# A new order for all operations of an attention and MLP kernel, and one more batch's Z from f16 parts

## The chip, the cores and the metric

The kernel runs on one core of one Trainium2 chip. The metric is the time of one execution on the device, in microseconds (us); lower is better. The core has five engines that run side by side, each in the order of its own instructions: TensorE (PE in the profile, with its weight loads as PEld), VectorE (DVE), ScalarE (ACT), GpSimd (POOL), and SyncE (SP), which only issues DMA transfers here. An engine waits for another one by semaphores.

## The reference

Two attentions, one after the other, for 8 batches of 8 heads with 576 positions of 64 elements, and then an MLP over the 4608 rows of all batches:

```python
p_packed = sm_attn(p, k, v)                 # 32 packed queries attend to 576 keys
out = sm_attn(q, p_packed, p_packed)        # 576 queries attend to the 32 packed rows
x = out.transpose(0, 2, 1, 3).reshape(B * S, H * D)        # 4608 x 512
h = x @ w_in                                # 512 x 1024
e = np.exp(h - h_max)
solu = h * (e / (e.sum(-1) + 1e-9))
ln = (solu - mu) / np.sqrt(var + 1e-6) * g_ln
result = ln @ w_out                         # 1024 x 512
```

q, k, v, p and g_ln are float32, w_in and w_out float64, the result float32. sm_attn is a softmax of the scaled products, with 1e-9 added to the sum, times the values.

## The kernel before, in words

**Folding.** The second attention's output is never built. Since x @ w_in = (weights of the second attention) @ (p_packed @ w_in), the kernel multiplies the packed rows of a batch by w_in once, which gives Z (256 rows of 8 heads x 32, by 1024), and the first product of the MLP becomes (softmax weights, 576 x 256) @ Z. To keep float32's accuracy at f16 speed on PE, a float32 factor is split into a high and a low f16 part, and a product is the sum of three f16 products (high by high, high by low, low by high).

**A batch.** `attention(b)` (line 396) names its operations, all with /b behind: `lk0`, `lk1` load K with the packed queries in two halves, `lq0`, `lq1` load Q, `lv` loads V. `s10`, `s11` are the scores' two halves on PE, `mx` their row maxima (DVE), `mb` a bias, `ex` the exponentials (ACT), `ri`, `rs` the inverse sums. The exponentials are turned either on PE (`tp0` to `tp2`, copied by `tc0` to `tc2`) for the first three batches or, from `E16` = 3 on, split into f16 parts (`eh`, `el`), turned by a DMA (`et`) and joined (`ea`). `av` is the product with V on PE, `pp` scales it, `pe` and `pk` find its largest value, `pt` turns it on PE and `pc` copies it out; `un` and `uq` set the scales of the batch. `sx0`, `sx1` are the second attention's scores, `sb` a transpose by 32x32 blocks on DVE, and `sm`, `su`, `se`, `ss`, `si`, `sr`, `sn`, `at` the softmax over blocks of 32; `ah`, `al` split the result into f16 parts. Batch 0 does this softmax in two halves (`su0`, `su1` and so on). `z0`, `z1` are the two halves of Z on PE; `zh0`, `zl0`, `zh1`, `zl1` split them into f16 parts on their way out of PSUM.

**Where Z gets its factors.** For b < `Z16` a half of Z is one float32 product of the packed rows with w_in (line 596); from `Z16` on it is three f16 products. That needs w_in in f16 parts, made once (`zw0` to `zw3`, line 258, the high parts; `zy0` to `zy3`, line 261, the low parts, written over the float32 ones), and the batch's packed rows in two parts (`ph`, line 606, and `pl`, line 610). The four `zy` must come after the last float32 Z and before the first f16 Z:

```python
        if b < Z16:
            terms = [(st['ppT'], w_in_sb)]
        else:
            terms = [(st['ph'], w_hi), (st['ph'], w_lo), (st['pl'], w_hi)]
```

**A tile of rows.** `token_tile(i)` (line 693) names the operations of 128 output rows, with -i behind: `m1` is the first product (two PSUM banks; 12 matmuls of 512 columns), `nm` the row maximum (DVE), `nb` a bias, `bd` a bound (two small operations), `ex` the exponential (ACT), `u` the product with h and the sum (DVE), `mu` the mean, `yh` and `yl` the f16 parts of u, `tr` their transpose by DMA, `sq` the sum of squares (ACT), `ca` and `cr` the row's factor (POOL), `m2a` and `m2b` the two halves of the second product (12 matmuls each), `ev` the scaling out of PSUM, `st` the store. Every fifth tile or so lies across two batches and copies their scales first (`uc`).

**The weights.** w_in and w_out arrive as float64 words (`lw0` to `lw3`, `lW0` to `lW3`, 1 MB each), and `wa` (ACT), `wl`, `wm` (DVE) make float32 of them. `wp`, `wb0`, `wb1`, `wb` and `pw0`, `pw1`, `pw` find their scales, `cs` and `cv` the column means of g_ln * w_out, `ct` subtracts them (eight operations on DVE), `ch` and `cl` split the result into f16 parts for the second product. The raw words live in buffers that belong to others later (`W_HOME`, line 28). `hw` are fillers: two matmuls each that nobody reads.

**The order.** `ORDER` (line 29) lists every operation once. `perform` (line 364) issues them in that order, checks that what each needs stands ahead of it and that buffers and PSUM banks are free, and ties the instructions of each engine to one another, so that every engine, SP with its DMAs too, runs its share in exactly this order. A letter behind the colon is the engine of an operation that several could do (v DVE, p POOL, a ACT; without one, the usual engine of that operation), a digit is the first PSUM bank of a matmul group (0 to 5 are three pairs; 6 and 7 single). So `zw3/w:a` is done by ACT and `m1-4:0` writes banks 0 and 1. An operation waits for its inputs, for its engine's operation ahead, and for whoever last held its bank or buffer: a bank pair of `m1-i` is freed by `u-i`, of `sx` by `sb`, of `z` by `zl`, of `s1` by `ex`.

Of the kernel before, what the change touches and what calls it, by code (L numbers as in the profile page):

```python
# [899 lines left out]
```

## Time and profile before

| | |
|---|---|
| median of 3 runs | 377.14 us (377.0 to 378.87) |
| the profiled execution | 375.99 us, its span 374.2 us |
| mean granted clock of PE | 0.986 |
| busy share PE, DVE, ACT, POOL | 95%, 76%, 55%, 58% |
| HBM read, written | 38.80 MB, 9.44 MB |

The span goes from the first to the last instruction; the execution has 1.8 us around it. Times in the views count from the span's start. A busy share is of the time an instruction occupies its engine. Matmuls overlap and their ends are modelled: a row of PE in the chain of waits gives the time by which a group moved its end, and 12 matmuls of 512 f16 columns move it by 2.59 us when they run without a hole. PEclk is the granted clock of PE, 1.00 for 2.4 GHz and 0.50 for 1.2 GHz.

### The profile page before, as it was taken

Reading aid. Unit: us, or ns where it says so; the run is one execution under the profiler, and the core shown is the slowest. Engines: PE = TensorE matmul, PEld = TensorE weight load, DVE = VectorE, ACT = ScalarE, POOL = GpSimd, SP = SyncE. Lnnn points to the kernel's source line nnn. Section 1 sums busy time; section 2 is a strip of 40 time slices with the busy share of each in tenths; the row PEclk is TensorE's granted clock in tenths of the full one; section 3 lists DMA queues with packets and bytes.
Section 4 is the critical chain, followed back from the end, with each engine's and each line's share of the span. In section 5 each row is a group of like instructions: output and inputs, shape, how many; then the busy total and the mean of one; then the engine's idle time right before and its main releaser. Section 6 shows DMA issues by size and latency. Waiting matters only on the chain.

```text
span 374.2 us, 7628 instructions
## 1 busy us (share of the span) xinstructions
PE 356.7 (95%) x3013; PEld 168.1 (45%) x3013; DVE 283.5 (76%) x419; ACT 206.9 (55%) x346; POOL 218.1 (58%) x315
## 2 busy tenths in 40 slices
...
GB/s 288 420 424 428 310 261 194 276 284 208 347 184 238 254 141 197 265 234 191 91 145 152 196 80 107 122 163 70 170 56 0 134 93 87 168 52 145 114 197 57
DMA packets 99349, 70.56 MB, mean 189 GB/s; under 512 B 88049, under 2 KB 88049, under 8 KB 97777
## 3 DMA queue, kind: packets, MB, share of 16 engines
...
q8 instruction: 23, 0.38, 0.4%
...
HBM read 38.80 MB, written 9.44 MB: 129 GB/s over the span
## 4 chain that ended last, share of the span: by engine, by line
PE 69%; DVE 13%; DMA 7%; POOL 4%; ACT 3%; issue 3%; SPq 1%; ACTq 0%; DVEq 0%; POOLq 0%
PE pa L789 32%; PE ps L723 20%; PE ps L789 8%; DMA yT<-yhl 4%; DMA v<-in_v_dram 3%; PE ps L604 2%; PE pa L504 2%; POOL yhl L763 2%; PE ps L436 2%; PE ps L538 1%; DVE w_in_sb L199 1%; DVE yhl L323 1%; DVE u L752 1%; DVE nm L729 1%; DVE zl L622 1%
## 5 line engine op out<-in xcount | busy, mean ns | idle before, releaser
L789 PE MATMUL pa<-wch,yT 128*128 128x512 f16 x416 | 129.2, 379 | 1.6 <-DMA yT<-yhl 1.6
L789 PEld LDWEIGHTS <-yT 128*128 128x128 f16 x864 | 83.6, 98 | 104.0 <-DMA yT<-yhl 3.4
L789 PE MATMUL pa<-wcl,yT 128*128 128x512 f16 x208 | 78.8, 379 | 0.0
L763 POOL TENSOR_TENSOR yhl<-u,yhl 128x1024 f16<-128x1024 f32 x22 | 48.6, 2207 | 20.1 <-ACT yhl L148 11.1
L729 DVE TENSOR_REDUCE nm<-ps 128x1 f32<-128x1024 f32 x36 | 43.8, 1218 | 19.1 <-PE ps L723 17.3
L752 DVE SCALAR_TENSOR_TENSOR u<-e,s_row,ps 128x1024 f32<-128x1024 f32 x36 | 45.4, 1270 | 16.4 <-ACT e L747 10.5
L747 ACT ACTIVATE e<-ps,bias,unit 128x1024 f32<-128x1024 f32 x36 | 43.3, 1202 | 23.1 <-DVE bias L144 21.3
L723 PE MATMUL ps<-zh,a2h 128*128 128x512 f16 (+1 forms) x160 | 54.8, 381 | 0.5 <-DVE rs L465 0.5
L723 PE MATMUL ps<-zl,a2h 128*128 128x512 f16 (+1 forms) x160 | 54.6, 379 | 0.0
L723 PE MATMUL ps<-zh,a2l 128*128 128x512 f16 (+1 forms) x160 | 54.6, 379 | 0.0
L789 PE MATMUL ps<-wch,yT 128*128 128x512 f16 x160 | 49.6, 379 | 0.0
L723 PEld LDWEIGHTS <-a2h 128*128 128x128 f16 (+1 forms) x320 | 27.7, 100 | 35.7 <-issue 4.7
L771 ACT ACTIVATE e<-u,negmu 128x1024 f32<-128x1024 f32 x36 | 41.1, 1141 | 3.4 <-POOL negmu L144 2.6
L148 ACT CAST yhl<-u 128x1024 f16<-128x1024 f32 x22 | 22.9, 1041 | 19.5 <-DMA yT<-yhl 13.0
L740 POOL TENSOR_SCALAR bound<-nm,unit 128x1 f32<-128x1 f32 x25 | 13.4, 536 | 33.5 <-DVE nm L729 33.4
L781 POOL TENSOR_SCALAR c_row<-sq,k_out,s_eps 128x1 f32<-128x1 f32 x36 | 19.6, 544 | 19.6 <-ACT e L771 19.2
L789 PE MATMUL ps<-wcl,yT 128*128 128x512 f16 x80 | 30.3, 379 | 0.0
L142 ACT ACTIVATE o_sb<-pa,c_row 128x512 f32<-128x512 f32 x17 | 11.6, 683 | 32.3 <-PE pa L789 24.1
L782 POOL TENSOR_TENSOR c_row<-c_row,neg_half 128x1 f32<-128x1 f32 x36 | 21.3, 590 | 3.0
L775 POOL TENSOR_SCALAR s_eps<-se,s_row 128x1 f32<-128x1 f32 x36 | 13.3, 369 | 16.2 <-DVE s_row L742 8.7
L723 PEld LDWEIGHTS <-a2l 128*128 128x128 f16 (+1 forms) x160 | 14.3, 100 | 16.8
L763 DVE TENSOR_TENSOR yhl<-u,yhl 128x1024 f16<-128x1024 f32 x14 | 19.9, 1424 | 0.1
...
## 6 DMA issues: line engine op xcount, KB each, us to landing
...
```

The costliest lines, as they stand in the source:

```text
L148: nc.scalar.copy(out, in_)
L723: nc.tensor.matmul(h[rows, 512 * n:512 * n + 512], lhsT=lhsT, rhs=z[:, r, 512 * n:512 * n + 512], start=t == 0, stop=t == end)
L729: nc.vector.tensor_reduce(out=nm, in_=st['h'], axis=AX.X, op=ALU.max, negate=True)
L740: eng.tensor_scalar(out=bound, in0=st['nm'], scalar1=st['nm'], scalar2=st['unit'][:, 2:3], op0=ALU.mult, op1=ALU.max)
L747: nc.scalar.activation(st['e'], st['h'], AF.Exp, bias=st['bias'], scale=st['unit'][:, 1:2], accum_out=st['se'])
L752: nc.vector.scalar_tensor_tensor(out=st['u'], in0=st['e'], scalar=st['s_row'], in1=st['h'], op0=ALU.mult, op1=ALU.mult, accum_out=st['su'])
L763: engines[on(f'yl-{i}', 'v')].tensor_tensor(out=st['y'][:, 1], in0=st['u'], in1=st['y'][:, 0], op=ALU.subtract)
L771: nc.scalar.activation(st['e'], st['u'], AF.Square, bias=st['negmu'], accum_out=st['sq'])
L775: nc.gpsimd.tensor_scalar(out=s_eps, in0=st['se'], scalar1=1e-09, scalar2=st['s_row'], op0=ALU.add, op1=ALU.mult)
L781: nc.gpsimd.tensor_scalar(out=c_row, in0=st['sq'], scalar1=k_out[:, 0:1], scalar2=s_eps, op0=ALU.mult, op1=ALU.add)
L782: nc.gpsimd.tensor_tensor(out=c_row, in0=c_row, in1=neg_half, op=ALU.pow)
L789: nc.tensor.matmul(st['po'], lhsT=st['yT'][:, a, c], rhs=w[:, c], start=c == 0 and t == 0, stop=c == NFC - 1 and t == 2)
```

## The change

All 1119 words of ORDER change their places, many their engine or bank, and two words come in (`ph/2`, `pl/2`); there are nine fillers instead of ten. `Z16` goes from 3 to 2, so that batch 2's Z is made of three f16 products too, which needs the four `zw` and `zy` ahead of `z0/2`. The loads stand in another order: the second part of w_in ahead of the first K, V ahead of K's second half for batch 1, the rest of w_in ahead of w_out, Q of batch 1 ahead of batch 3's K. The functions stay as they are. The diff, cut to the start, the stretch with the four `zy`, and the end:

```diff
-Z16 = 3
+Z16 = 2
...
 ORDER = '''
-hw28/w:6 lg/w lw0/w lk0/0 s10/0:0 mx0/0 lk1/0 s11/0:2 lk0/1 hw42/w:7 lk1/1 mb0/0:p wa0/w lv/0 hw23/w:6 hw18/w:7 mx1/0
-mb1/0:v wl0/w:v wm0/w lq0/0 lq1/0 lW0/w ex0/0 ex1/0 lw2/w lw1/w tp0/0:6 tp1/0:7 tp2/0:0 tc0/0:v s10/1:4 ri/0:a tc1/0:a
-tc2/0:v av/0:6 mx0/1 mb0/1:p ex0/1 s11/1:2 rs/0 pp/0:v pt/0:7 pe/0 pc/0:a sx0/0:0 mx1/1 sx1/0:4 mb1/1:a sb0/0 sb1/0
-sm0/0 ex1/1 ri/1:p tp0/1:6 tp1/1:0 sm1/0 su1/0:v wl4/w:v tp2/1:1 hw40/w:2 wa4/w tc0/1:a su0/0:p se0/0 ss0/0 si0/0:v gx/w
-se1/0 wa2/w wl2/w:a sr0/0 sn0/0:p wm4/w cs0/w:6 wp4/w:3 wl1/w:a wp0/w:2 wm2/w lw3/w wa1/w at0/0 ss1/0 lW2/w wm1/w pk/0
-wa3/w tc1/1:a wl3/w:v lW1/w wm3/w tc2/1:v wl6/w:v cs1/w si1/0:p wp1/w wa6/w wp2/w wp3/w hw37/w:0 wb0/w wb1/w wl5/w:a
-rs/1 wm6/w lW3/w sr1/0 wa5/w z0/0:4 wa7/w z1/0:0 wb/w un/0 zh1/0:a cs4/w sn1/0:p cs5/w wm5/w wp5/w wp6/w wl7/w:v at1/0
-cs2/w cs3/w zh0/0:a wm7/w zl1/0 wp7/w pw0/w zl0/0 cs6/w pw1/w pw/w cs7/w ah1/0:a ah0/0:a lv/1 al0/0:p al1/0:p ko/w lk0/2
-s10/2:0 mx0/2 lk1/2 cv/w:a av/1:7 s11/2:4 m1-2:2 mb0/2:a pp/1:a ex0/2 ct0/w lk0/3 ct1/w ch0/w:a lk1/3 mx1/2 m1-1:0
-mb1/2:a uq/0 gd/w ct4/w ct5/w ct2/w ex1/2 tp0/2:6 ct3/w nm-2 ch2/w:a cl0/w:p ch1/w:a m1-0:4 nb-2:a ex-2 ri/2:a pe/1
-bd-2:p nm-1 nb-1:v lk0/4 cl1/w:p pt/1:7 bd-1:v ex-1 ca-1 u-2 pk/1 tc0/2:a u-1 mu-1:p pc/1:a ct6/w yh-1:a rs/2 tp1/2:6
-lq0/1 sx0/1:2 tc1/2:a lq1/1 m1-3:0 yl-1:p sq-1 ct7/w nm-0 nb-0:a tp2/2:6 tc2/2:a bd-0:p sb0/1 ex-0 sx1/1:2 nm-3 bd-3:p
-lv/2 sb1/1 u-0 un/1 av/2:6 nb-3:a ex-3 lk1/4 z0/1:2 ch3/w:a s10/3:4 zh0/1:a pp/2:a u-3 tr-1 m2a-1:7 cl2/w:p cl3/w:p
-lq0/2 yh-3:a yl-3:p sm/1 su/1:v se/1 mx0/3 mb0/3:a lv/3 ex0/3 pe/2 s11/3:0 mx1/3 mb1/3:a ex1/3 ss/1 mu-0:p cr-1 zl0/1
-pt/2:6 pc/2:a si/1:p m2b-1 sr/1 sn/1:v at/1 ev-1:a eh/3:a z1/1:4 zh1/1:a uq/1 uc-4 tr-3 yh-2:a ah/1:a yh-0:a el/3:p
...
-el/4:p m2b-0 ev-2:a u-5 ca-5 ex-7 u-7 rs/3 s10/5:2 z0/2:4 mx0/5 av/3:7 tr-4 z1/2:0 tr-6 ev-0:v mb0/5:a si/2:p sr/2 ex0/5
-zh1/2:a zw1/w:p pp/3:v zl1/2 sn/2:p at/2 yh-8:a yl-8:v st-0 s11/5:2 mx1/5 mu-7:a yh-7:a yl-7:p m2a-4:6 zh0/2:a zl0/2
-pt/3:7 pc/3:v pe/3 cr-6 m2a-6:0 m2b-4 zw0/w:a zy0/w et/4 m2b-6 ca-8 lq0/4 ea/4:p st-2 pk/3 mb1/5:a un/3 mu-8:a sq-8
-sx0/3:4 ah/2:a lq1/4 al/2:p sb0/3 ex1/5 tr-7 eh/5:a ev-6:a el/5:p sx1/3:2 s10/6:0 uq/3 sb1/3 ri/4:a ev-4:a mx0/6 rs/4
-mb0/6:a ex0/6 s11/6:4 mx1/6 sm/3 av/4:7 su/3:v pp/4:a mb1/6:v ex1/6 m1-9:2 nm-9 bd-9:v ca-7 sq-7 cr-7 lk0/7 yh-5:v
-yl-5:p m1-11:0 lv/5 nb-9:a ph/3:a tr-8 cr-8 se/3 st-4 nm-11 nb-11:a ex-11 ss/3 bd-11:p m2a-7:6 si/3:p ca-11 zy3/w u-11
-zw2/w:p ex-9 u-9 zy1/w m1-10:4 nm-10 mu-5:v pt/4:7 et/5 m2b-7 yh-9:a yl-9:p m2a-8:0 bd-10:p tr-5 m1-12:2 eh/6:v el/6:v
-m2b-8 nb-10:a mu-9:p m2a-5:1 lq0/5 ev-7:v nm-12 ri/5:a pc/4:a mu-11:v pe/4 bd-12:p sr/3 sn/3:p zy2/w nb-12:v pk/4 tr-9
...
-tr-33 st-27 ca-34 cr-34 tr-31 ca-35 m2a-33:6 m2b-33 ev-28:a st-28 m2a-31:7 u-35 yh-35:v yl-35:v st-25 tr-35 ev-34:v
-m2b-31 ev-33:a st-33 mu-31:p mu-35:v yh-32:v yl-32:p tr-32 m2a-35:6 m2b-35 m2a-32:0 ca-32 m2b-32 sq-35 ca-31 mu-32:v
-sq-31 cr-31 st-34 ev-31:v st-31 cr-35 ev-35:a st-35 hw32/w:7 hw36/w:6 hw8/w:7 hw13/w:6 sq-32 cr-32 ev-32:a st-32 zz/7
+lg/w hw1/w:6 lw0/w hw25/w:7 gx/w wa0/w wl0/w:v wm0/w lw2/w wa2/w wl2/w:a lk0/0 hw9/w:6 s10/0:0 mx0/0 lk1/0 s11/0:2
+mb0/0:v ex0/0 mx1/0 mb1/0:a ex1/0 lk0/1 lv/0 hw10/w:7 lk1/1 tp0/0:6 tp1/0:7 tp2/0:0 lq0/0 lq1/0 s10/1:4 lw1/w lw3/w
+lW0/w lW2/w tc0/0:a wm2/w ri/0:a rs/0 lW1/w tc1/0:a tc2/0:a av/0:6 pp/0:v pe/0 s11/1:2 pt/0:7 mx1/1 pc/0:a mx0/1 sx0/0:0
+sb0/0 sm0/0 mb0/1:p ex0/1 lW3/w hw29/w:6 su0/0:p sx1/0:0 sb1/0 sm1/0 su1/0:p wl1/w:v mb1/1:a ex1/1 tp0/1:6 tp1/1:0 pk/0
+se0/0 wa1/w tc0/1:a ss0/0 si0/0:a wa3/w wm1/w hw2/w:1 tc1/1:a wp0/w:6 wp1/w wp2/w tp2/1:2 wl3/w:v sr0/0 sn0/0:p se1/0
+wm3/w wp3/w at0/0 wb0/w wb1/w tc2/1:a ss1/0 wb/w z0/0:4 z1/0:0 si1/0:p sr1/0 sn1/0:p wl4/w:a wa4/w wm4/w wa6/w wl6/w:a
+ri/1:p un/0 wm6/w ah0/0:a uq/0 wa5/w wl5/w:v wm5/w cs0/w:6 cs1/w wp4/w:7 lk0/2 cs4/w cs5/w cs2/w zh0/0:a zw3/w:p at1/0
+cs3/w lk1/2 wp5/w s10/2:2 zl0/0 wl7/w:a wp6/w wa7/w rs/1 zh1/0:a wm7/w mx0/2 ah1/0:a lv/1 wp7/w pw0/w al0/0:p al1/0:p
+s11/2:4 pw1/w zl1/0 lq0/1 lq1/1 pw/w mx1/2 cs6/w cs7/w cv/w:a mb0/2:a ko/w gd/w ct0/w ct1/w ct4/w mb1/2:a m1-1:0 ct5/w
+nm-1 ex0/2 av/1:7 m1-2:2 lk0/3 bd-1:p ct2/w ex1/2 ri/2:p ch0/w:a pp/1:a ct3/w ct6/w ch2/w:a nb-1:a ch1/w:a cl1/w:p ex-1
+ct7/w tp0/2:6 lv/2 nm-2 tc0/2:a bd-2:p u-1 m1-3:4 nm-3 nb-2:a ex-2 u-2 tp1/2:7 cl2/w:p pt/1:6 tc1/2:a pc/1:a yh-1:a
+tp2/2:7 bd-3:p yl-1:p pe/1 s10/3:0 mu-1:a tc2/2:a mx0/3 sq-1 mb0/3:a sx0/1:2 sb0/1 ex0/3 rs/2 ch3/w:a pk/1 un/1 lk1/3
+lk0/4 av/2:7 pp/2:v cl0/w:p sx1/1:2 sb1/1 ca-1 nb-3:a s11/3:0 mx1/3 ex-3 mb1/3:a pt/2:6 sm/1 m1-0:2 lq0/2 u-3 nm-0
+su/1:p lk1/4 bd-0:p ex1/3 eh/3:a tr-1 lq1/2 yh-3:a yl-3:p nb-0:v z0/1:0 z1/1:4 cl3/w:v cr-1 se/1 tr-3 ss/1 m2a-1:7
+zh0/1:a zl0/1 zh1/1:a lk0/5 el/3:p et/3 ex-0 pc/2:a zl1/1 si/1:a sr/1 m2b-1 ev-1:a s10/4:0 s11/4:4 u-0 yh-0:a mx0/4 ca-3
+m2a-3:7 sn/1:v pe/2 yl-0:p pk/2 m2b-3 ca-2 mu-3:a mb0/4:a ex0/4 mu-2:a at/1 ah/1:a mx1/4 mb1/4:a al/1:v sx0/2:2 sb0/2
+uq/1 sx1/2:0 ex1/4 un/2 sb1/2 ea/3:p ri/4:v m1-4:4 uc-4 nm-4 ri/3:a sm/2 eh/4:a zz/0 el/4:p bd-4:v zw1/w:a sq-3 cr-3
+nb-4:v ex-4 yh-2:v yl-2:p mu-0:p sq-2 tr-0 m1-7:2 nm-7 ev-3:a u-4 st-1 ca-0 nb-7:a rs/3 lv/3 ex-7 bd-7:v lk1/5 lq0/3
+zy1/w u-7 su/2:p yh-4:a m2a-0:6 mu-7:p m1-8:0 sq-0 cr-0 ca-7 s10/5:4 mx0/5 tr-2 av/3:7 zw2/w:a se/2 nm-8 mb0/5:a bd-8:p
+lq1/3 yl-4:p m2b-0 ev-0:a st-3 zy3/w yh-7:a ex0/5 lv/4 m1-6:2 pp/3:v pt/3:7 uq/2 ss/2 si/2:p nm-6 nb-8:a m2a-2:6 ex-8
+ca-8 s11/5:4 yl-7:v u-8 mu-8:v cr-2 sq-7 mu-4:a tr-7 sq-4 mx1/5 m2b-2 pe/3 ph/2:a nb-6:a ex-6 pk/3 zy2/w zw0/w:v ev-2:a
+pl/2 zy0/w tr-4 bd-6:p m1-5:0 nm-5 et/4 pc/3:v mb1/5:a ex1/5 u-6 lk0/6 m2a-7:6 lk1/6 yh-8:a st-0 z0/2:4 z1/2:2 zh0/2:a
+yl-8:p un/3 ph/3:a sq-8 sr/2 sn/2:v at/2 m2a-4:7 m2b-7 nb-5:a ea/4:v bd-5:p cr-7 m2b-4 uq/3 lk0/7 yh-6:v zh1/2:a zl1/2
+sx0/3:2 st-2 mu-6:v ah/2:a al/2:p eh/5:a ex-5 u-5 zz/1 ev-7:a lq0/4 yl-6:p av/4:6 rs/4 zl0/2 sb0/3 sx1/3:0 el/5:p
+s10/6:4 pp/4:a sb1/3 sm/3 tr-6 ca-4 mx0/6 mu-5:a s11/6:2 ca-5 mx1/6 lv/5 m1-9:0 cr-4 pl/3 ev-4:a st-4 m2a-6:6 nm-9
...
+yh-32:v m1-35:2 ca-28 m2a-30:7 tr-33 nb-34:a ex-34 mu-28:a sq-28 cr-28 m2a-33:0 bd-34:v u-34 ca-34 ev-28:a st-28 cr-30
+m2b-30 m1-31:4 zz/7 yh-34:v yl-34:p m2b-33 yl-32:v tr-34 uc-31 nm-31 tr-32 m2a-34:6 ev-30:v ca-32 nm-35 nb-35:v sq-32
+nb-31:v ev-33:v m2b-34 cr-32 m2a-32:7 ex-35 mu-34:p sq-34 zz/6 st-33 bd-35:p u-35 bd-31:p mu-35:p st-30 yh-35:v cr-34
+ca-35 yl-35:v m2b-32 ex-31 tr-35 m2a-35:0 m2b-35 u-31 yh-31:a ev-34:a st-34 yl-31:v tr-31 m2a-31:6 mu-31:v sq-31 m2b-31
+sq-35 cr-35 ev-35:a ev-32:v st-32 hw33/w:7 hw27/w:7 st-35 hw31/w:7 ca-31 cr-31 ev-31:a st-31
 '''
```

## Rows read from the trace of the kernel before

**Rows 1.** The page: busy us, share and instructions of each engine.
```profile
PE 356.7 (95%) x3013; PEld 168.1 (45%) x3013; DVE 283.5 (76%) x419; ACT 206.9 (55%) x346; POOL 218.1 (58%) x315
```

**Rows 2.** Windows by stage: from:to, length, busy us of each engine, clock, DMA.
```profile
0.00:46.43 46.43, 35.81 (x438) 21.48 (x442) 31.99 (x66) 24.61 (x34) 10.09 (x23) 0.89 0.92 377
46.43:67.28 20.85, 17.36 (x245) 8.17 (x235) 20.59 (x34) 17.46 (x34) 15.15 (x17) 1.00 0.75 224
67.28:82.04 14.76, 14.76 (x149) 6.21 (x151) 13.80 (x15) 12.55 (x22) 12.28 (x16) 1.00 0.84 288
82.04:109.45 27.41, 27.41 (x266) 12.67 (x264) 23.42 (x36) 19.66 (x36) 22.96 (x36) 1.00 0.89 246
109.45:124.24 14.79, 14.65 (x212) 7.08 (x197) 13.54 (x17) 11.35 (x18) 13.65 (x10) 1.00 0.95 258
124.24:370.46 246.22, 244.95 (x1737) 111.89 (x1734) 180.10 (x256) 120.59 (x202) 143.93 (x218) 1.00 0.57 135
370.46:374.20 3.74, 1.73 (x9) 0.59 (x6) 0.00 (x0) 0.69 (x1) 0.00 (x0) 1.00 0.18 70
```

**Rows 3.** Waits of PE: line, waited for, us in total, times, longest.
```profile
PE ps L604 <- DVE u L752: 0.7, 1, 0.7
```

**Rows 4.** Chain of waits, in order of time: start, us, what.
```profile
3.92 11.45 DMA v<-in_v_dram
...
62.00 5.21 DMA yT<-yhl
...
82.06 5.41 PE ps L723 x36
...
106.24 0.86 PE ps L604 x16
...
108.35 1.10 PE ps L604 x16
...
124.28 5.29 PE ps L723 x24
...
153.12 1.44 PE ps L604 x46
```

**Rows 5.** Timeline of the start: start, us, engine, line, operation, tiles, shapes, idle before.
```profile
7.86 0.72 PE L436 MATMUL ps<-kT 64*32 64x288 f32 x16 [1.27 <-DMA kT<-in_k_dram]
...
12.93 0.68 DVE L150 COPY e1T<-pa 128x512 f32<-128x512 f32 x1
...
17.59 1.21 PE L436 MATMUL ps<-kT 64*32 64x288 f32 x16
17.71 0.61 DVE L144 TENSOR_SCALAR pp<-pa,rs 128x128 f32<-128x128 f32 x2 [3.16 <-PE pa L504]
...
23.44 1.16 DVE L566 TENSOR_TENSOR s<-s,mx 128x576 f32<-128x576 f32 x1
...
24.52 0.68 DVE L188 TENSOR_SCALAR u<-kT 128x1024 int32<-128x1024 int32 x1
...
46.43 1.41 DVE L323 SCALAR_TENSOR_TENSOR yT<-yT,gs,o_sb 128x512 f32<-128x512 f32 x2
```

**Rows 6.** Groups by line: tiles, shapes, count, busy us, mean ns, idle before.
```profile
L763 DVE TENSOR_TENSOR yhl<-u,yhl 128x1024 f16<-128x1024 f32 x14 | 19.9, 1424 | 0.1
...
L262 DVE SCALAR_TENSOR_TENSOR w_in_sb<-w_in_sb,w_pow,w_hi 128x1024 f16<-128x1024 f32 x4 | 7.1, 1779 | 0.0
...
L144 DVE TENSOR_SCALAR zh<-ps 128x1024 f16<-128x1024 f32 x5 | 6.1, 1220 | 7.5 <-PE ps L604 7.5
...
L144 POOL TENSOR_SCALAR w_hi<-w_in_sb,w_pow 128x1024 f16<-128x1024 f32 x2 | 5.7, 2871 | 0.1
...
L612 DVE SCALAR_TENSOR_TENSOR pl<-ppT,unit,ph 128x256 f16<-128x256 f32 x5 | 2.6, 513 | 0.0
```

**Rows 7.** Windows of the start in which PE's clock was granted at half.
```profile
15.77:19.19 3.42, 3.42 (x94) 2.17 (x82) 1.17 (x4) 0.00 (x0) 0.00 (x0) 0.50 1.02 419
...
26.00:32.84 6.84, 5.21 (x21) 3.06 (x22) 6.74 (x12) 5.95 (x7) 3.07 (x2) 0.50 1.01 413
```

70 lines of the change are left out of this document (33 added, 37 removed).

## The prediction, made before the change was run

> **What bounds the kernel now.** I read the page's busy line first, then the windows by stage, then the waits of TensorE (PE), then the timeline and the chain of waits where those pointed. The busy line puts PE at 95% and VectorE (DVE) at 76% of the span [rows 1], an average that hides three stages [rows 2]. Up to 67.28 us PE has holes (35.81 of 46.43 us and 17.36 of 20.85 us busy, and some of that is slow or overlapping matmuls) while DVE is nearly full in the second piece (20.59 of 20.85). From 67.28 to 124.24 PE has 0.14 us of idle time and DVE is 89% busy: 13.80 + 23.42 + 13.54 = 50.76 of 56.96 us. From 124.24 to 370.46 PE is idle for 246.22 - 244.95 = 1.27 us, over half of it in the one wait of [rows 3], and DVE has a quarter of its time free. The last 3.74 us are one scaling and one store. So the time is: where the dense stretch begins, plus a fixed amount of matmuls, plus small stalls, plus a tail. Nothing that moves work off ScalarE (ACT) or GpSimd (POOL) late in the kernel can be worth more than 1.27 us; the startup and the DVE load up to 124 us decide.
>
> **Two checkpoints.** I counted each engine's operations in both orders. When m1-4 begins (82.06 us before [rows 4]) PE has run exactly the same matmuls in both, fillers aside. When m1-9 begins (124.28 us) it has run one second product, m2-7, in place of another, m2-6: the same amount. At m1-9 the durations of the operations listed ahead sum to 107.7 us on DVE before and 107.8 after, 99.2 and 99.2 on ACT, 68.1 and 70.1 on POOL (164, 143 and 98 instructions in the trace up to there; the sums overcount by up to 4%, DVE's busy time up to there being 31.99 + 20.59 + 13.80 + 23.42 + 13.54 = 103.3 us [rows 2]). So the change is judged by when PE reaches these two points.
>
> **Part A: DVE's load before m1-4 falls by 2.5 us.** Leaving DVE for ACT or POOL, or moved behind: one of batch 0's subtractions su1/0 (1.16), three weight shifts wl4, wl6, wl7 (0.68 each), the copies tc0/0 (0.68) and tc2/0, tc2/1 (0.28 each), four operations of 0.15 to 0.42 us (0.96), and su/1 (1.36): 6.8 us. Arriving: wl1, wl5 (0.68 each), pp/2 (0.61), four small ones (0.98) and cl3: 2.95 + cl3 [rows 5]. A subtraction of cl3's shape has no row on DVE; yl on DVE has the same shape and type (1.42), and a PSUM read of that size is 1.22 [rows 6]; I take 1.3 of 1.2 to 1.5. Sum: 4.25 - 6.8 = -2.5 us. The work goes to ACT, which has 46.43 - 24.61 us free in the first stretch, and to POOL, with 36 us free [rows 2]. Both run in order: zw3, now on POOL at 2.87 [rows 6], stands ahead of al0/0 and al1/0; I get al1/0 done at 42.7 us against m1-1's turn at 45.1, so it is hidden by 2.4 us; gone that cover, m1-1 is late by what is over.
>
> **Part B: batch 0 starts later, +1.0 us.** The second 1 MB of w_in (lw2) now goes ahead of the first K. At 419 GB/s [rows 7] it takes 2.5 us, so K's wait, which ended at 7.86 [rows 5], ends at about 10.3. V, landed at 3.92 + 11.45 = 15.37 [rows 4], gets 2.45 us of lw2 ahead and loses K1's second half (0.59 MB, 1.4 us): 16.4. The first pp/0 on DVE moves from 17.71 [rows 5] to about 18.7. In exchange wm2 is done before it, and lw1, lw3 land ahead of the four pieces of w_out. Bounds: 0 if DVE uses the early weights fully, +2.5 if K's delay goes all the way through; 1.0 is the V path, which ends last.
>
> **Walking the chain with these numbers.** From pp/0 at 18.7 DVE has 26 us of listed work up to the scale pw, and waits about 1.5 us (for wa3, sn0/0, wb1): the first ct at 46.2, before 46.43 [rows 5]. m1-1 starts at 45.1, m1-2 at 48.9, m1-3 at 52.2. nm-1 now stands ahead of the last four ct, so u-1 ends at 56.0, yh-1 at 58.5, yl-1 at 60.7 and its transpose, 5.21 as at 62.00 [rows 4], at 66.0. PE meanwhile does s11/3, pt/2 and z1/1 too (2 us that came after m2a-1 before), the last waiting for u-3's bank until 66.1, and begins m2a-1 at 67.4 (before 67.25). m2a-3 must wait for its transpose (yl-3 behind bd-0 on POOL, landing about 74.6), which gives back 0.5 to 0.7 us of the lead. On SP the Q loads of batch 1 pass ahead of K3; Q, K and V all land before their turn in this walk. m1-4 then starts at 81.0: A, B and this wait are -2.5 + 1.0 + 0.5 = **-1.0 us**.
>
> **Part C: batch 2's Z in f16, -0.5 us on PE.** A half of Z in float32 takes 0.86 to 1.10 (x16), two f16 halves 1.44 together [rows 4]: 2 x 0.97 - 1.44 = -0.5. It adds ph/2 on ACT (0.5) and pl/2 on DVE (0.51), and z0/2 now waits for both and for the four zy, 1.78 us each [rows 6], on DVE, which stand after z1/2 in the order now and ahead of it then. zw0 goes to DVE, for which there is no row: between 0.68 (tc0, half its columns [rows 5]) and 1.22 (zh, as many from PSUM [rows 6]); I take 0.9. Queued behind a late z0/2 on PE are z1/2, m2a-4, m2b-7 and all that follows. Between m1-4 and m1-9 DVE thus has 40.9 us of listed work instead of 38.7, in 41.7 us instead of 42.2; its idle time there, 42.20 - 23.42 - 13.54 = 5.2 us now, falls to about 2.5. By the walk zy0 ends at 108.3 and PE arrives at z0/2 at 109.8: hidden, by 1.5 us. At m1-9 the last bank is freed at 122.4 and PE comes at 122.7.
>
> **The rest: 0.** From m1-9 on PE has the same work. The shortest stretch of PE work between a first product and its second product late in the kernel is 17 us (m1-29; 18 for m1-31), against 13 before (m1-35); the latency of that path is nm 1.2, exp 1.3, u 1.3, two halves 2.3 and the transpose 3.7 to 5.2, 10 to 12 us. Bounds: -1.0 (all stalls gone) to +3 (two of them each as long as a half transpose). The last tile changes from 32 to 31, but what follows the last matmul is still one scaling and one store: 3.74 us [rows 2]. Three fillers in place of four lie beside that store.
>
> **Sum.** -1.0 - 0.5 = -1.5 us on the profiled execution: span 374.2 to 372.7, 375.99 to 374.5 with the 1.8 us around the span. The median of the runs, 377.14, is 1.15 above that execution: **375.6 us**.
>
> **The clock.** PE was granted half of its clock, 1.2 GHz, from 15.77 to 19.19 and from 26.00 to 32.84 [rows 7], the first time right after it had waited for V until 15.37; s1 took 1.21 us in it instead of 0.72 [rows 5]. I kept half the clock for batch 0's product with V, so the sum holds what a drop there costs. The Trainium skill's page "TensorE: Matmul & The Clock Gate", section "HAM oscillation — how this bites in real kernels", describes short bursts of matmuls between waits for DMAs that start at the lower clock each time. The drop at 15.77 agrees with it, and it speaks against this change, whose wait for the first K grows: that is rival 2.
>
> **Rivals.**
> 1. *Only Z counts.* DVE works off its list as late as before; A and B cancel: 377.14 - 0.5 = 376.6. For it: both orders carry 107.8 us of DVE work up to m1-9. Against: the lighter list before m1-4. 0.12.
> 2. *The lower clock comes earlier.* With an idle stretch of 3 us in place of 1.27 ahead of the first K, PE falls to 1.2 GHz before s1: the first s1 (+0.5), the turns (+0.3, in the same ratio) and some of the weights' products come later on DVE's path, about +1.1: 376.7. 0.04.
> 3. *DVE can't take the four zy so early* (the other side). Place: z0/2. If no zy finds a hole in DVE's list, 7.1 - 1.5 = 5.6 us of stall, 381.2; if DVE only keeps the idle time it has now in this stage, zy0 ends 2.7 us later, 1.2 over the margin, 376.8. I take 379.8. It decides from a PE wait at z0/2 to m1-9 of over 3.4 us in all. For it: DVE is 94% full there in the walk. Against: four of DVE's large operations of this stage go to POOL and two to ACT. 0.22.
> 4. *K's delay goes through.* B is +2.5, and A is lost in ACT's queue: 377.14 + 2.5 - 0.5 = 379.1. For it: ACT's list up to the first ct grows by 1.5 us. Against: DVE has the second weight to work on while it waits. 0.07.
> 5. *More gain.* The listed DVE durations overcount by 4%, 4 us by m1-9, so the walk is late by up to 2 us wherever DVE leads: 375.6 - 2.0 = 373.6. Against: the transposes and PE's own work then hold m1-4. 0.25.
>
> **How the numbers follow.** The forecast has 0.30, with its own range of 374 to 377. About 0.5% (1.9 us) is what a measurement of this kernel can tell from no change: under 375.25 is faster, over 379.03 slower. Faster: rival 5 and two fifths of the forecast, 0.25 + 0.12 = 0.37. Slower: rival 4, two thirds of rival 3 and a tenth of the forecast (late stalls), 0.07 + 0.15 + 0.03 = 0.25. Same: 0.38. The range goes from rival 5 with 1.6 us beyond it to most of rival 3's upper end: 372.0 to 380.3.
>
> **What would show it.** In the profile after: K's first wait ending near 10.3; the first ct near 46; m2a-1 near 67.4; m1-4 near 81.0 and m1-9 near 122.7; no PE wait over 1 us at z0/2. Wrong if m1-4 starts after 82, if DVE work holds PE between z0/2 and m1-9, or if PE's idle time after m1-9 is over 3 us.

## The result, and the profile after the change

The changed kernel takes 372.78 us (median of 4 runs, 372.56 to 374.12) beside 377.07 us for the kernel before (376.07 to 378.87): 0.9888 of its time, 95% interval [0.9844, 0.9933]. That is faster than the 375.6 us that were forecast: a gain of 4.3 us beside a forecast one of 1.5. It lies inside the range, 0.8 us above its lower end of 372.0. Its profiled execution took 372.9 us, span 371.1.

The page's busy line, the windows by stage, PE's longest wait and pieces of the chain, all of the changed kernel; columns as in [rows 1 to 4].

```profile
PE 354.9 (96%) x3027; PEld 165.9 (45%) x3027; DVE 278.9 (75%) x421; ACT 209.1 (56%) x357; POOL 214.7 (58%) x304
```

```profile
0.00:47.32 47.32, 35.41 (x388) 19.31 (x389) 30.38 (x61) 26.72 (x41) 17.40 (x26) 0.93 0.97 396
47.32:66.95 19.63, 18.61 (x316) 9.38 (x315) 19.44 (x34) 18.63 (x38) 15.98 (x16) 1.00 0.61 217
66.95:80.67 13.72, 12.94 (x121) 5.54 (x117) 11.93 (x14) 11.14 (x21) 13.14 (x15) 1.00 0.73 172
80.67:122.66 41.99, 41.99 (x481) 19.59 (x477) 37.25 (x59) 30.08 (x52) 37.08 (x43) 1.00 0.85 255
122.66:367.38 244.72, 244.70 (x1733) 111.69 (x1734) 179.93 (x258) 121.85 (x207) 131.11 (x207) 1.00 0.56 140
367.38:371.07 3.69, 1.29 (x6) 0.39 (x4) 0.00 (x0) 0.69 (x1) 0.00 (x0) 1.00 0.18 71
```

```profile
PE ps L436 <- DMA kT<-in_k_dram: 4.0, 2, 3.4
```

```profile
74.19 2.76 PE pa L789 x12
...
80.70 5.41 PE ps L723 x36
...
109.83 1.44 PE ps L604 x48
...
122.66 2.72 PE ps L723 x12
```

What to see: m1-4 begins 1.36 us earlier (80.70 for 82.06 [rows 4]); m1-9 at 122.66 for 124.28; the stretch behind it is 244.72 us for 246.22 [rows 2], with 0.02 us of idle time on PE where there were 1.27; the wait of [rows 3] is gone, and after 75 us PE has no wait worth a row. The tail is the same. 1.36 + 0.26 + 1.5 = 3.1 us is the difference of the spans.

The changed kernel ran again in two later sets of runs (e4, e12 below). These are its checkpoints beside those of the experiments, from the starts of the first matmuls of m1-4 and m1-9 and the end of the last second product in each trace (us):

| | m1-4 | m1-4 to m1-9 | m1-9 to the last product | median of runs | ratio to before |
|---|---|---|---|---|---|
| before | 81.98 | 42.23 | 246.25 | 377.07 | 1 |
| after | 80.63 | 42.00 | 244.75 | 372.78 | 0.9888 |
| e4 (after) | 79.68 | 42.01 | 244.90 | 372.05 | 0.9870 |
| e12 (after) | 80.53 | 42.01 | 244.64 | 372.22 | 0.9882 |
| e1 new head, old tail | 81.80 | 43.86 | 246.50 | 377.99 | 1.0026 |
| e2 old head, new tail | 87.24 | 42.01 | 245.24 | 379.19 | 1.0053 |
| e3 old, two waits removed | 82.53 | 42.22 | 245.68 | 376.23 | 0.9977 |
| e5 old engines in the start | 94.05 | 42.01 | 245.43 | 386.73 | 1.0230 |
| e6 first K ahead | 81.22 | 42.00 | 244.69 | 372.38 | 0.9860 |
| e7 float32 Z | 79.63 | 44.67 | 247.47 | 379.35 | 1.0052 |
| e8 fillers | 79.57 | 42.01 | 245.02 | 372.52 | 0.9856 |
| e9 float32 Z, zy in the holes | 80.42 | 44.00 | 246.71 | 376.52 | 0.9993 |
| e10 wb0 ahead | 80.02 | 42.01 | 244.55 | 372.48 | 0.9886 |
| e11 wb0 ahead, fillers | 80.92 | 42.00 | 245.04 | 373.43 | 0.9910 |

A ratio has an interval of some 0.25 to 0.45% to either side, so the small steps are read from the traces. The first three columns are of the one execution that was profiled, the last two of all runs.

### The profile page after: what moved, and what is told of

Its sections match the earlier page's. It is cut to its first block, busy times and chain, and to the rows that moved or that the text cites. A ratio compares the mean times of both kernels' runs of the same rounds, so it can differ in the third digit from the quotient of the medians.

```text
span 371.1 us, 7650 instructions
## 1 busy us (share of the span) xinstructions
PE 354.9 (96%) x3027; PEld 165.9 (45%) x3027; DVE 278.9 (75%) x421; ACT 209.1 (56%) x357; POOL 214.7 (58%) x304
## 4 chain that ended last, share of the span: by engine, by line
PE 83%; DVE 7%; DMA 6%; POOL 3%; issue 1%; ACT 0%; SPq 0%; POOLq 0%
PE pa L789 41%; PE ps L723 23%; PE ps L789 8%; DMA qT<-in_q_dram 4%; PE ps L604 3%; PE ps L538 2%; PE pa L316 1%; PE pa L504 1%; DMA zh<-in_moe_w_in_dram 1%; POOL wcl L329 1%; PE ps L436 1%; DVE u L752 1%; DVE zl L622 1%; DVE nm L729 1%; DVE yT L323 1%; POOL s L586 1%
## 5 line engine op out<-in xcount | busy, mean ns | idle before, releaser
L789 PE MATMUL pa<-wch,yT 128*128 128x512 f16 x480 | 149.5, 379 | 0.8 <-ACT yhl L148 0.8
L789 PE MATMUL pa<-wcl,yT 128*128 128x512 f16 x240 | 91.0, 379 | 0.0
L763 POOL TENSOR_TENSOR yhl<-u,yhl 128x1024 f16<-128x1024 f32 x23 | 51.2, 2227 | 21.2 <-ACT yhl L148 9.8
L740 POOL TENSOR_SCALAR bound<-nm,unit 128x1 f32<-128x1 f32 x22 | 18.9, 859 | 27.1 <-DVE nm L729 27.0
L789 PE MATMUL ps<-wch,yT 128*128 128x512 f16 x96 | 30.2, 379 | 0.0
L142 ACT ACTIVATE o_sb<-pa,c_row 128x512 f32<-128x512 f32 x22 | 14.9, 684 | 25.9 <-POOL c_row L782 9.2
L148 ACT CAST yhl<-u 128x1024 f16<-128x1024 f32 x20 | 20.7, 1041 | 15.3 <-DVE u L752 13.0
L781 POOL TENSOR_SCALAR c_row<-sq,k_out,s_eps 128x1 f32<-128x1 f32 x36 | 14.8, 411 | 20.1 <-ACT e L771 19.4
L775 POOL TENSOR_SCALAR s_eps<-se,s_row 128x1 f32<-128x1 f32 x36 | 14.5, 402 | 15.3 <-ACT e L747 12.2
L763 DVE TENSOR_TENSOR yhl<-u,yhl 128x1024 f16<-128x1024 f32 x13 | 17.6, 1354 | 2.3 <-ACT yhl L148 2.2
L789 PE MATMUL ps<-wcl,yT 128*128 128x512 f16 x48 | 18.2, 379 | 0.0
## 6 DMA issues: line engine op xcount, KB each, us to landing
kT<-in_k_dram SPq DMA_DIRECT2D x8, 576.0 KB, 10.3
```

The costliest lines, as they stand in the source:

```text
L142: nc.scalar.activation(out, in_, AF.Copy, scale=scale)
L148: nc.scalar.copy(out, in_)
L740: eng.tensor_scalar(out=bound, in0=st['nm'], scalar1=st['nm'], scalar2=st['unit'][:, 2:3], op0=ALU.mult, op1=ALU.max)
L763: engines[on(f'yl-{i}', 'v')].tensor_tensor(out=st['y'][:, 1], in0=st['u'], in1=st['y'][:, 0], op=ALU.subtract)
L781: nc.gpsimd.tensor_scalar(out=c_row, in0=st['sq'], scalar1=k_out[:, 0:1], scalar2=s_eps, op0=ALU.mult, op1=ALU.add)
L789: nc.tensor.matmul(st['po'], lhsT=st['yT'][:, a, c], rhs=w[:, c], start=c == 0 and t == 0, stop=c == NFC - 1 and t == 2)
```

## The experiments

### Halves of the two orders: e1, e2, and the whole again, e4

e1 takes the words ahead of m1-4 from the new order and the others, with their engines and banks, from the old one; e2 the other way round.

```diff
 e1: new order up to m1-4 | then lv/3 mu-0:p uc-4 yh-2:a yl-2:p ... m1-4:0 tr-2 nm-4 ... (old), Z16 = 3
 e2: old order up to m1-4 | then et/3 un/2 ea/3:p ri/4:v m1-4:4 nm-4 ... (new), Z16 = 2
```

> The words ahead of m1-4 in the new order, with the new engines; from m1-4 on the old order and engines, and batch 2's Z in float32. Theory (three parts that add: the start 1.4 us, Z 0.2, late stalls 1.5): m1-4 begins at 80.6 us as in the changed kernel, the tail keeps the waits of 0.5 us ahead of m1-18 and 0.7 us ahead of z1/7, span 372.8, ratio to before 0.996. Rival (one cause: the early start puts VectorE's list ahead, and the late waits go with it): m1-4 at 80.6, no late wait, span 371.5 or less, ratio 0.992. Second rival (all of it is in the tail): m1-4 at 82, span 374.2.

> The words ahead of m1-4 in the old order; from m1-4 on the new order and engines, and batch 2's Z of f16 parts. Theory: m1-4 at 82.0 us, no PE wait after it, 290.5 us from there to the end, span 372.5, ratio to before 0.9955; with the run above the two reductions add up to that of the whole change. Rival (one cause, the early start): with the old start VectorE is 1.4 us later against the same list, so waits come back in the tail, above all at z0/2 (the four zy) and span is 374 or more. Second rival (all of it is in the tail): 371.1.

> The changed kernel itself, again, as the yardstick for the two halves. Theory (the spans tell the gain, and the profiled execution of the kernel before was a lucky one by some 1.1 us): ratio 0.9917, that is -3.1 us. Rival (the runs gain more than the profiled executions): ratio 0.9888, -4.2 us.

None of the theories on the halves came true as a whole: e2 is slower than either whole kernel, and e1 can't be told from the kernel before (1.0026, interval 0.9999 to 1.0054). Waits of PE after 70 us in e1 (the first fence) and in e2, and last the wait that is left in e2 after 124.3 us:

```profile
PE ps L723 <- DVE s L560: 1.8, 1, 1.8
PE pa L789 <- DMA yT<-yhl: 1.5, 1, 1.5
...
PE ps L723 <- DVE rs L465: 0.8, 1, 0.8
PE ps L604 <- DVE u L752: 0.7, 1, 0.7
```

```profile
PE pa L789 <- DMA yT<-yhl: 3.1, 2, 2.5
PE ps L723 <- DVE unit L252: 1.1, 1, 1.1
...
PE pa L789 <- DMA yT<-yhl: 0.6, 1, 0.6
```

In e1 the new head reaches m1-4 at 79.98, and then m1-4 waits 1.8 us: the old order gives it banks 0 and 1, which the new head has just used for sx1/2, and sb1/2 must read them first. Then m2a-2, which the old order has early, waits 1.5 us for a transpose that the new head has not begun. In e2 un/2 stands between VectorE's old list and m1-4 (1.1 us), after a wait of 2.5 us for a transpose. Its m1-4 is 5.3 us later than that of the kernel before, and these waits are not all of it: PE's granted clock was 0.50 from 58.25 to 61.66 and from 78.73 to 82.14 in this execution, where the kernel before has 1.00, and two products there took 4.12 and 4.45 us (m1-3 at 58.82, m2a-3 at 77.92) instead of 2.6 to 2.7. Four other runs of e2, at a mean clock of 0.991, have a median of 378.3 us, beside 376.0 of the kernel before at the same clock, so a loss of some 2.3 us is left. The seam thus costs more than either half brings, and the two runs can't show whether the halves add up. The stretch behind m1-9 does follow its own order, wherever it begins: the old tail takes 246.50 us in e1 with its two waits, now 0.8 and 0.7 us, and the new one 245.24 in e2 with one of 0.6. That part of the first theory stands: the tail's 1.5 us go with the tail's order, and not with the start.

e4, at 0.9870 [0.9825, 0.9915], lies beyond both theory (0.9917) and rival (0.9888), and only the rival's value is inside the interval: against the 376.5 us of before's runs beside it, 4.5 us are gained, while its own span is 3.9 us shorter than the one of [rows 2]. The runs gain more than the two profiled executions show, as the rival said; two reasons, an offset and the clock, are told in the section on the prediction.

### The late waits: e3

```diff
-... sx0/5:0 cr-14 ev-14:v ri/6:p sb0/5 av/6:7 ...
+... sx0/5:0 sb0/5 cr-14 ev-14:v ri/6:p av/6:7 ...
-... ex-27 bd-27:v u-27 ca-27 m2a-25:5 ev-22:a pl/7 nm-28 ah/7:a ... ca-30 nb-28:v ex-28 ...
+... ex-27 bd-27:v nm-28 nb-28:v u-27 ca-27 m2a-25:5 ev-22:a pl/7 ah/7:a ... ca-30 ex-28 ...
```

> The old order with three words moved, all late and all on VectorE: sb0/5 stands ahead of ev-14 (frees the bank for m1-18 about 0.8 us sooner) and nm-28 and nb-28 stand ahead of u-27 (VectorE is idle there from 299.7 to 303.8; exp 28 and u-28 come about 1.7 us sooner and free the bank for z1/7). Nothing else is changed. Theory (late waits were worth their whole length on PE): both waits gone, 1.27 us less PE idle time after m1-9, span 372.9, ratio 0.9966. Rival (such a wait is given back: the next word on PE waits instead, for a transpose or another bank): idle time after m1-9 stays above 0.8 us and the span within 0.4 us of 374.2.

Half and half. Both waits are gone, but PE's waits after 124 us are now these:

```profile
PE pa L789 <- DMA yT<-yhl: 0.4, 1, 0.4
PE pa L789 <- ACT o_sb L142: 0.3, 1, 0.3
```

m2a-15, which stood behind m1-18, now waits for its transpose, and m2a-14 for a bank. Of the 1.27 us 0.57 came out at the last product (245.68 for 246.25); without its waits either tail is 244.6 to 245.0 us of matmuls. The span is the same only because this execution reached m1-4 0.55 us later.

### Step A alone: e5

```diff
-tc0/0:a tc2/0:a tc2/1:a su1/0:p su/1:p wl1/w:v wl4/w:a wl5/w:v wl6/w:a wl7/w:a zw3/w:p pp/2:v cl3/w:v ...
+tc0/0:v tc2/0:v tc2/1:v su1/0:v su/1:v wl1/w:a wl4/w:v wl5/w:a wl6/w:v wl7/w:v zw3/w:a pp/2:a cl3/w:p ...
```

> The changed order throughout; of the operations ahead of m1-4 the 23 whose engine differs between the two orders go back to the old one (VectorE takes su1/0, su/1, wl4, wl6, wl7, tc0/0, tc2/0, tc2/1 and small ones again, and gives wl1, wl5, pp/2, cl3 and small ones away; zw3 goes from GpSimd to ScalarE). Theory (the lighter list of VectorE is what brings m1-4 forward, step A, about 2.5 us of VectorE's time): ahead of the first ct VectorE has some 3 us more, of which up to 2 us fits in its waits there; first ct at 48 to 49 us instead of 46.3 to 47.3, m1-4 at 81.5 to 82.5 instead of 79.7 to 80.6, ratio to before about 0.992. Rival (between 31.5 and 46 us it is TensorE's own list, z0/0 to pw1, that leads, and VectorE only waits for it): first ct within 0.4 us of the changed kernel's, m1-4 too, ratio 0.987.

Far over the theory: m1-4 comes 14.4 us later than in e4, five times the VectorE time that was moved. What ScalarE does at the place in question, in e5 and then in the changed kernel (timeline; in brackets the idle time before, and what ended it):

```profile
20.52 0.74 ACT L454 ACTIVATE e<-ps,nmb 128x576 f32<-128x576 f32 x1 [1.10 <-POOL nmb L447]
...
24.39 1.12 ACT L142 ACTIVATE u<-zl 128x1024 int32<-128x1024 uint32 x1 [3.05 <-DMA zl<-in_moe_w_in_dram]
25.41 0.29 ACT L445 ACTIVATE nmb<-nmx,lift 128x1 f32<-128x1 f32 x1
25.73 0.74 ACT L454 ACTIVATE e<-ps,nmb 128x576 f32<-128x576 f32 x1
```

```profile
20.55 0.74 ACT L454 ACTIVATE e<-ps,nmb 128x576 f32<-128x576 f32 x1 [1.10 <-POOL nmb L447]
...
21.28 0.28 ACT L445 ACTIVATE nmb<-nmx,lift 128x1 f32<-128x1 f32 x1
21.59 0.74 ACT L454 ACTIVATE e<-ps,nmb 128x576 f32<-128x576 f32 x1
```

wl1, back on ScalarE, waits 3.05 us for its weight, and ex1/1 behind it comes 4.1 us later; tp1/1 on PE waits 3.2 us for that, and the first ct is at 51.5 instead of 46.3. So the price is not VectorE's sum alone, but also what stands behind a waiting operation on its engine. Nor is it this one wait alone. The first 5.2 us also come with a wait of PE of 2.4 us at 38.21 and a granted clock of 0.50 for 6.8 us from 24.16 and 3.4 us from 37.81, where e4 has 1.00. The other 9 us come with three more waits of PE (2.5 us at 68.75, 1.2 at 81.24, 2.2 at 88.53) and a clock of 0.50 for 3.4 us each from 68.53 and 89.01. Which letter brings which of them was not tested. An engine letter and its place in the list are one choice.

### Step B alone: e6

```diff
-lg lw0 gx wa0 wl0 wm0 lw2 wa2 wl2 lk0/0 s10/0 mx0/0 lk1/0 s11/0 ... ex1/0 lk0/1 lv/0 ... tc0/0 wm2 ri/0 rs/0
+lg lw0 gx wa0 wl0 wm0 lk0/0 s10/0 mx0/0 lk1/0 lw2 s11/0 ... ex1/0 wa2 wl2 lk0/1 lv/0 ... tc0/0 ri/0 wm2 rs/0
```

> The changed order, but the second weight lw2 is loaded after the first two pieces of K instead of ahead of them, and wa2, wl2, wm2 stand accordingly later (step B undone). Theory (K's 2.5 us of delay is hidden, since V, at 16.45 us, ends last either way): K's wait ends at 7.9 instead of 10.4, av/0 still starts at 16.6 and pp/0 at 18.0, first ct and m1-4 within 0.3 us of the changed kernel's, ratio 0.987 to 0.988. Rival (the prediction's step B: the delay costs 1.0): pp/0 at 17.0 and m1-4 1.0 us earlier. Second rival (the weight taken early is worth more than the delay): wm2 now falls into VectorE's busy stretch, m1-4 0.5 to 1.2 us later.

PE's timeline in e6 and in e4, the first scores and the first product with V:

```profile
7.80 0.72 PE L436 MATMUL ps<-kT 64*32 64x288 f32 x16 [0.64 <-DMA kT<-in_k_dram]
...
16.58 2.36 PE L504 MATMUL pa<-v,e1T 128*32 128x64 f32 x80 [2.51 <-DMA v<-in_v_dram]
```

```profile
10.23 0.72 PE L436 MATMUL ps<-kT 64*32 64x288 f32 x16 [2.40 <-DMA kT<-in_k_dram]
...
16.60 1.32 PE L504 MATMUL pa<-v,e1T 128*32 128x64 f32 x80 [0.68 <-DMA v<-in_v_dram]
```

K is ready 2.4 us sooner, and the product with V begins at the same moment, since V lands at 16.44 and 16.46. On this the theory holds: the delay of K is hidden behind V. The time (ratio 0.986) is the changed kernel's within the interval. But the first ct, at 47.95, and m1-4, at 81.22, come 0.6 us after those of the changed kernel's first profile and not within 0.3. Whether that is the second rival can't be judged from the trace: in this execution PE ran at half clock from 15.17 to 25.41, in which the product took 2.36 us instead of 1.32.

### Step C alone: e7 and e9

Both set Z16 = 3 and leave out ph/2 and pl/2; the four zy, which must then wait for z1/2, go behind zl1/2, u-5, nm-9, su/3 (e7), or ahead of sb1/3, ss/3, un/4, nm-10 (e9).

> The changed order with batch 2's Z in float32 again: ph/2 and pl/2 are left out, and the four zy stand after z1/2 (behind zl1/2, u-5, nm-9 and su/3). Theory (Z's f16 parts are worth what PE saves, 2 x 0.94 - 1.44 = 0.44 us, less 0.2 for the switches between float32 and f16): 0.2 to 0.45 us longer from m1-4 to the end, no wait at z0/2 or z0/3, ratio 0.0005 to 0.0012 above that of the changed kernel, not to be told in the times, only in the trace. Rival (the four zy, off VectorE's list ahead of m1-9, let other waits go): the same or shorter. Second rival (they come too late for z0/3): a wait of up to 3 us at z0/3.

> As the run with batch 2's Z in float32 before, but with the four zy put where the changed kernel's VectorE has its holes: ahead of sb1/3 (hole 0.89 us), ss/3 (1.03), un/4 (1.00) and nm-10 (1.13), 1.41 us each. Theory (the f16 parts are worth little on PE, 0.44 us, and much by place: after m1-9 VectorE has no room for 5.6 us more ahead of z0/3, which the new order starts 12 us earlier): the holes take 4.05 of 5.64 us, the rest is late; with no zy ahead of zl0/2 the 1.8 us wait at s10/6 goes, m1-9 at 122.1 to 122.4, last matmul 0.5 to 2.5 us later than in the changed kernel, ratio 0.989 to 0.994. Rival (it was only the place of the first zy): 0.2 to 0.5 us later, ratio 0.988. Second rival (float32 itself costs more than its matmuls): 4 us or more again.

PE's longest waits after m1-4, in e7 and in e9:

```profile
PE ps L436 <- DVE zl L622: 1.8, 1, 1.8
...
PE ps L723 <- DVE s L560: 1.5, 1, 1.5
```

From m1-4 to the last product e7 takes 5.4 us more (44.67 + 247.47 against 42.01 + 244.7) and e9 4.0: over the theory in both, and in e9 near the second rival's 4, though it isn't float32 that costs most of it. PE's own part is some 0.44 us (the two halves move its end by 1.88 us in e9's chain, by 1.44 as f16 parts). Most of the rest is waits for VectorE's work: the new order starts z0/3 at 141 us (153 before), and the four zy must now be done between z1/2 and there. PE waits 1.82 us at s10/6 in e7 and 1.5 at m1-9 in e9, and later at transposes and banks, 4.1 and 3.3 us in all from m1-4 on. And some of the zy cost more there. Durations of the four zy (min, median, max in ns, first and last start) in the kernel before, the changed one, e7 and e9:

```profile
L262 DVE SCALAR_TENSOR_TENSOR w_in_sb<-w_in_sb,w_pow,w_hi x4: 1306/1438/2934, 118.2 to 145.4; 128x1024 f16<-128x1024 f32 x4
```

```profile
L262 DVE SCALAR_TENSOR_TENSOR w_in_sb<-w_in_sb,w_pow,w_hi x4: 1390/1405/1411, 89.7 to 105.4; 128x1024 f16<-128x1024 f32 x4
```

```profile
L262 DVE SCALAR_TENSOR_TENSOR w_in_sb<-w_in_sb,w_pow,w_hi x4: 1404/1719/2974, 115.5 to 130.9; 128x1024 f16<-128x1024 f32 x4
```

```profile
L262 DVE SCALAR_TENSOR_TENSOR w_in_sb<-w_in_sb,w_pow,w_hi x4: 1393/1804/2579, 121.1 to 138.1; 128x1024 f16<-128x1024 f32 x4
```

The long ones run into a large GpSimd operation, as the last section shows; in the changed kernel none does. What a float32 Z with the best places would cost stays open; with two sets of places it is 4.0 and 5.4 us in the traces. By medians e9 is 4.3 us above e12, and e7 some 6.9 above e6 and e8: e7's profiled execution was its fastest, at a mean clock of 1.0, and its runs go up to 381.33.

### The start's lead and the clock: e8, e10, e11

```diff
 e8:  + two fillers ahead of wp0, one ahead of wp1, one ahead of wp3, two ahead of wb1
-... sr0/0 sn0/0 ... wp3 at0/0 wb0 wb1 tc2/1 ss1/0 wb z0/0 z1/0 si1/0 sr1/0 sn1/0 wl4 wa4 wm4 ...
+... sr0/0 sn0/0 ... wp3 wb0 at0/0 wb1 tc2/1 wb z0/0 z1/0 ss1/0 si1/0 wl4 wa4 wm4 sr1/0 sn1/0 ...   (e10)
 e11: e10 + two fillers ahead of wp0, one ahead of wp1, one ahead of wp3
```

> The changed kernel with six more fillers (two matmuls each, into a bank nobody reads) in the holes of TensorE between 24.5 and 31.5 us: two ahead of wp0, one ahead of wp1, one ahead of wp3, two ahead of wb1. Theory (in the first profile of the changed kernel the clock was 0.5 from 31.98 to 35.40, just when TensorE's own list leads, and that cost 0.8 of the 0.95 us by which its m1-4 is later than in the second profile; it falls after the holes): no half clock between 24 and 46 us in the profile or the other runs, m1-4 at 79.6 to 79.9, mean clock 0.995 or 1.0 in most runs, ratio 0.985 to 0.987. Rival (the fillers only delay the weights' products): m1-4 0.3 to 0.6 us later, clock as before. Second rival (the clock falls whatever TensorE does): half clock in that stretch again, no change.

> The changed kernel with VectorE's short wb0, which TensorE's wb1, z0/0 and all up to m1-1 wait for, ahead of at0/0, which waits for GpSimd's sn0/0; wb and wm4 also ahead of batch 0's small ones (ss1/0, sr1/0). Theory (between 31.3 and 45.4 us TensorE's own list leads, so what starts it earlier comes out at the end): wb1 at 30.5 instead of 31.3, m1-1 0.7 to 0.9 us earlier, m1-4 0.6 to 0.9 earlier (about 78.9 at full clock), time 0.6 to 0.9 us below the changed kernel's, ratio about 0.985. Rival (VectorE's list leads, it carries the same work): wb1 earlier, first ct and m1-4 where they were.

> The run before with four more fillers between 24.5 and 29 us: two ahead of wp0, one ahead of wp1, one ahead of wp3. Theory (they keep the clock up through the stretch that TensorE leads): no half clock between 24 and 46 us, mean clock 0.995 in half of the runs or more, median 0.2 to 0.5 us below that of the run before. Rival (the clock falls there in few executions anyway): the same median within 0.2 us.

> The changed kernel itself, the yardstick for the three runs before on the same chip. Expected: 372.0 to 372.9 us, ratio 0.986 to 0.989, TensorE without a wait after m2a-3.

PE's timeline from wb1 on in e4, in the first profile of the changed kernel, and in e10:

```profile
31.33 0.49 PE L214 MATMUL pa<-ident,w_peak 128*128 128x128 f32 x2 [1.37 <-DVE w_peak L211]
...
31.75 1.95 PE L604 MATMUL ps<-w_in_sb,ppT 64*32 64x512 f32 x32
...
34.39 1.98 PE L316 MATMUL pa<-yT,g_mean 128*128 128x512 f32 x4 [0.70 <-DVE unit L252]
```

```profile
31.52 0.49 PE L214 MATMUL pa<-ident,w_peak 128*128 128x128 f32 x2 [1.36 <-DVE w_peak L211]
...
31.94 3.62 PE L604 MATMUL ps<-w_in_sb,ppT 64*32 64x512 f32 x32
```

```profile
30.37 0.49 PE L214 MATMUL pa<-ident,w_peak 128*128 128x128 f32 x2 [0.39 <-DVE w_peak L211]
30.79 1.95 PE L604 MATMUL ps<-w_in_sb,ppT 64*32 64x512 f32 x32
34.09 1.98 PE L316 MATMUL pa<-yT,g_mean 128*128 128x512 f32 x4 [1.35 <-DVE yT L199]
```

e10's wb1 and Z come 1.0 us sooner than e4's, and the next operation takes it back: cs0 waits for wm4 on VectorE (1.35 us, the last row). First ct at 46.70, m1-4 at 80.02: the rival was right, PE's list did not lead alone, and the median is 372.48 beside the 372.22 of e12. VectorE is busy for 13.4 of the 14.5 us from 31.5 to 46 (13.5 in e4), so its own list leads here. The loads may hold it from behind as well: they move at 424 GB/s through this stretch, and wa6 on ScalarE begins at 32.00 (31.95 in e4), when its weight has just landed. No run takes the two apart.

The fillers gave nothing: e8's median is that of the others, and e11's is 1.2 us over e12's. There the first products of the weights came later for the fillers (wb1 at 31.24 for 30.37). e8's profile has no half clock after 17.8 us, as its theory said, but nor have e4's and e7's, without fillers; its runs, all at a mean clock of 0.991 or 0.995, are no proof. No version beat the changed kernel.

## Why the prediction was right, and where its sum was wrong

**Direction and checkpoints.** The two points by which the change was to be judged came out as walked: m1-4 80.63 (81.0 forecast, 81.98 before), m1-9 122.63 (122.7). K's wait ended at 10.40 (10.3), m2a-1 began at 66.92 (67.4), zy0 ended at 106.78 (108.3) and z0/2 began without a wait at 109.76 (109.8). m2a-3 waited 0.8 us (0.5 to 0.7). Rival 3, the four zy coming too late, did not happen: they took 5.6 us instead of 7.1. Nor did rival 1, as m1-4 came earlier, nor rival 4, as e6 shows. Rival 5's 373.6 is nearer to the result than the forecast, but by luck: it had DVE's listed durations make the walk late by up to 2 us, and its times are only 0.4 us after the trace's at m1-4 and 0.1 at m1-9.

**A and B: -1.36 instead of -1.0, by other reasons.** In e4, which kept its full clock, the gain at m1-4 is 2.3 us. B's +1.0 was +0.26 at pp/0 (17.97 for 17.71): V landed when forecast (16.45), but the product with V ran at full clock, 1.32 us, where the walk kept half. A was priced as VectorE's sum; e5 shows that taking these letters back costs 14 us in this order, through queues and stretches at half clock, so no run shows the -2.5 by itself, and what else makes up m1-4's gain is argued and not shown. The walk also had VectorE lead up to the first ct, at 46.2. That is what e4 does, at 46.32. In the first profile it came at 47.32; there VectorE waited 0.8 us longer for the scores s10/2, behind the half-clock stretch of PE that is told below. VectorE's row in the first profile, and in e4:

```profile
42.64 0.76 DVE L440 TENSOR_REDUCE nmx<-ps 128x1 f32<-128x576 f32 x1 [1.00 <-PE ps L436]
...
41.64 0.76 DVE L440 TENSOR_REDUCE nmx<-ps 128x1 f32<-128x576 f32 x1 [0.20 <-PE ps L436]
```

**C: -0.2 to -0.3 at m1-9 instead of -0.5.** The two halves move PE's end by 1.44 us where they moved it by 0.86 and 1.10 [rows 4], 0.5 as reckoned; where the other half of that went is not shown. And the step left out what the edit permits: the zy may go ahead of z0/2 only if batch 2 is f16, and against the two other sets of places of e7 and e9 this is worth 4.0 to 5.4 us in the new order. Counted on PE alone, the term had the right sign and missed the point.

**"The rest: 0" is the term that was mis-sized, by 1.5 us.** Its bound was -1.0, "all stalls gone"; the stalls were 1.27 us, all gone, and the matmuls 0.2 shorter. e1 and e2 show that this belongs to the tail's order, and e3 that two such waits removed by hand bring 0.57 and not 1.27, as the next in line wait instead. Here a whole new order did what two moves did not.

**The offset of 1.15 us did not carry over.** It is the other large error of the sum. It was added because the profiled execution of before (375.99) lay under its median. Sorted by mean granted clock, 29 runs of before at 0.986, its own, have a median of 376.64, and 22 at 0.991 one of 376.03; so that execution was fast for its clock. The changed kernel's was at its own median. With 374.5 and no offset the forecast would have been 1.7 us off, the late stalls.

**The clock, which stood in the sum as unchanged.** PE's granted clock was 0.50 from 15.77 to 19.19 and for 6.84 us from 26.00 [rows 7]; in the changed kernel from 11.50 to 14.92, before V has landed, and from 31.98 to 35.40:

```profile
11.50:14.92 3.42, 3.04 (x22) 1.24 (x22) 2.44 (x4) 1.76 (x4) 0.00 (x0) 0.50 1.04 439
31.98:35.40 3.42, 3.42 (x33) 0.64 (x32) 3.14 (x14) 3.35 (x4) 2.01 (x2) 0.50 1.04 427
```

The second falls on batch 0's Z: 3.62 us instead of e4's 1.95 (the fences above). Where a half-clock stretch falls there (after, e12, e9), m1-4 comes at 80.4 to 80.6; where none does (e4, e7, e8), at 79.6 to 79.7: 0.9 us. Of 63 runs of before none had a mean clock over 0.991; of 16 runs of the changed kernel six had 0.995 or 1.0, and the four at 1.0 have a median of 372.0, the seven at 0.991 one of 372.7. This can be part of what the runs gain beyond 3.1 us. Rival 2, a lower clock that costs, had the sign wrong: 6.8 us at half clock in the first profile, 10.3 in the kernel before. The Trainium skill's "TensorE: Matmul & The Clock Gate", section "HAM oscillation — how this bites in real kernels", puts such drops down to waits for DMAs between short bursts of matmuls. Here the four waits from 24 us up to wb1 were as long in e4, which kept its clock (1.62, 0.57, 0.85 and 1.37 us), as in the first profile, which lost it (1.16, 0.56, 0.86 and 1.36). Earlier ones were not: 3.36 us for K and 1.53 for Q in the first profile, 2.40 and none in e4. What decides in one execution stays open.
